# Convolution and state-space heads on one core: a 64x64 transform in array tiles, with shared rings and a written-out order

## The chip, the cores and the metric

The kernel runs on one core of a Trainium2 chip. The metric is device time in microseconds (us), from start to end of one launch; smaller is better. A core has five engines that run side by side: TensorE (PE in the profile; PEld is its loading of weights), VectorE (DVE), ScalarE (ACT), GpSimd (POOL) and SyncE (SP). In this kernel the last two issue nearly all DMAs. Matmuls write to PSUM, which has eight banks of 128 x 512 fp32 here; ACT and DVE bring the results from there to SBUF.

## The reference

Two independent heads, each on a sequence of S = 2048 positions and D = 1024 channels, in bf16. Their results stand side by side in the output.

```python
# head A
k_shift = sum over t < 4 of k_pad[:, t:t+S, :] * shift_k[:, 3 - t]
kv = k_shift * v
y = irfft(rfft(kv, 2S) * rfft(ssm_k, 2S))[:S] + kv * ssm_D
a = q * y
# head B
Lam_bar = exp(dt * Lam);  Bu = x @ B_bar.T          # complex
h[t] = Lam_bar * h[t-1] + Bu[t]
b = 2 * real(h @ Cmat.T) + x * Dskip
```

## The kernel before, in words

**Head B** works through 16 chunks i of 128 positions. `U(i, jp)` (L579, matmuls at L588) makes a quarter of Bu with 32 matmuls of 128x128 by 128x128 on PE; `ue` (L590) copies it out on ACT. On DVE a chunk then goes through `r1` (L600, rotation by a table, into the product tile mt), `r2` (L609, L611, adds, and the carry from the chunk before), `sc` (two scans at L618, and the next carry at L622 and L623), `r3` (L600 again, rotation back) and `r4` (L630). `y(i, dh, part)` (L634, matmuls at L641, skip term at L646) multiplies with C in eight parts, two halves dh of four, each half in one PSUM bank; `ye` (L656) and `yst` (L658) copy and store it. The chain over the chunks is sequential on DVE through the carry. Before the first U all of B must be loaded (`bl`, L556), transposed on PE (`bT`, L553) and copied (`bc`, L564); C likewise (`cl`, `cT`, `cc`, L572) before the first y. `x` (L576) loads a chunk of x through a transposing DMA.

**Head A** is a 4096-point transform split as 256 x 16, in three stages with a round trip through DRAM between each two.

- Stage 1, 16 residues n2. `k` (L660) and `v` (L670) load one residue, 128 rows 16 positions apart, with one DMA of 256 KB each; `kvm` and `kva` (L675 to L691) form kv on DVE; `am(n2, w)` (L695, L698) multiplies by the constant F1t in four matmuls 128x128 by 128x512; `ae` (L707) copies; `ast` (L709) stores 256 KB to Ys_kv. For ssm_k the same: `hl`, `hT` (L722), `hc` (L730), `hd`, `hm` (L742, two matmuls of 256 columns), `he` (L750), `hst` (L757) into Ys_h.
- Stage 2, 32 groups g. `l` (L760) loads two groups of both spectra and their weight tile wts, all in one step, into a ring of three (`l2`). `sh` and `sk` (L772) transform, `she` (L779) and `ske` (L785) copy, `sw` (L790, L791) swaps real and imaginary halves by two SBUF-to-SBUF DMAs, `pr` (L796) multiplies, `sa` (L805) transforms back, `sae` (L817) copies, `vst` (L819) stores to Vs.
- Stage 3, 16 residues. `vl` (L824) loads both halves of Vs, `ql` (L829) q, `a3` (L836) is four matmuls 128x128 by 128x512, `a3e` (L844) copies, `qm` (L848) multiplies by q, `ost` (L850) stores.

Every load of spectra in stage 2 waits for all of stage 1's stores; every `vl` waits for all `vst`.

**What sets the order.** `make_plan` (L174) lists each step as a task with an engine, a duration, dependencies, buffers taken and given back, and a due time `pr`. `Plan.run` (L88) plays this through and gives the list in which the steps are emitted. Each engine and each DMA queue then runs its own part of that list strictly in order.

**Buffers.** PSUM is split into four pools: ps_t 2 banks, ps_u 2, ps_y 1, ps_a 3. SBUF has a pool per kind of tile (for example u 5, xT 8, h 2, ld 5, ysb 3, hab 4, vv 4), some of them opened only for their stage, and one product tile mt that `r1`, `r3` and `kvm` share.

Of the kernel before, what the change touches and what calls it, by code (L numbers as in the profile page):

```python
# [15 lines left out]
F32 = mybir.dt.float32  # L16
# [5 lines left out]
N1, N2, NFFT = 256, 16, 4096  # L22
NG = 32


def a_constants():
    n1 = np.arange(128)[:, None]; k1 = np.arange(128)[None, :]
    ang = 2 * np.pi * n1 * (k1 + 0.5) / N1
    F1 = np.stack([np.cos(ang), -np.sin(ang)], axis=1)
    G = np.stack([np.cos(ang.T) * 2 / NFFT, -np.sin(ang.T) * 2 / NFFT], axis=1)  # L30
    s = np.arange(4)[:, None, None, None]; g = np.arange(NG)[None, :, None, None]
    n2 = np.arange(N2)[None, None, :, None]; k2 = np.arange(N2)[None, None, None, :]
    kk1 = 32 * s + g
    phi = 2 * np.pi * n2 * (2 * kk1 + 1 + 2 * N1 * k2) / (2 * NFFT)
    cph, sph = np.cos(phi), np.sin(phi)
    W2 = np.zeros((2, 4, N2, NG, 2, 4, N2))
    Wa = np.zeros((2, 4, N2, NG, 2, 4, N2))
    Wb = np.zeros((2, 4, N2, NG, 2, 4, N2))
    for si in range(4):
        c_ = cph[si]; s_ = sph[si]  # L40
        c_n2k2 = np.transpose(c_, (1, 0, 2)); s_n2k2 = np.transpose(s_, (1, 0, 2))
        W2[0, si, :, :, 0, si, :] = c_n2k2
        W2[1, si, :, :, 0, si, :] = s_n2k2
        W2[0, si, :, :, 1, si, :] = -s_n2k2
        W2[1, si, :, :, 1, si, :] = c_n2k2
        c_k2n2 = np.transpose(c_, (2, 0, 1)); s_k2n2 = np.transpose(s_, (2, 0, 1))
        Wa[0, si, :, :, 0, si, :] = c_k2n2
        Wa[0, si, :, :, 1, si, :] = s_k2n2
        Wa[1, si, :, :, 0, si, :] = -c_k2n2
        Wa[1, si, :, :, 1, si, :] = -s_k2n2  # L50
        Wb[0, si, :, :, 0, si, :] = -s_k2n2
        Wb[0, si, :, :, 1, si, :] = c_k2n2
        Wb[1, si, :, :, 0, si, :] = -s_k2n2
        Wb[1, si, :, :, 1, si, :] = c_k2n2
    f = lambda a: np.ascontiguousarray(a.reshape(128, -1), dtype=np.float32).astype(ml_dtypes.bfloat16)
    W2 = np.transpose(W2, (0, 2, 1, 3, 4, 5, 6))
    Wa = np.transpose(Wa, (0, 1, 2, 3, 4, 6, 5))
    Wb = np.transpose(Wb, (0, 1, 2, 3, 4, 6, 5))
    W3 = np.stack([W2.reshape(128, NG, 128), Wa.reshape(128, NG, 128), Wb.reshape(128, NG, 128)], axis=2)
    return f(F1), f(G), f(W3)  # L60


class Task:
    __slots__ = ("name", "eng", "dur", "lat", "deps", "acq", "rel", "pr", "idx", "nd", "succ", "after", "asucc", "t0", "t1", "nbytes")


COLD = 14.0
LAT = {"PE": .25, "ACT": .2, "DVE": .15, "SP": 0.0, "POOL": 0.0}


class Plan:
    def __init__(self, caps, rate=310e3, dlat=1.6):
        self.T, self.order, self.caps, self.rate, self.dlat = {}, [], dict(caps), rate, dlat

    def add(self, name, eng, dur, deps=(), acq=(), rel=(), pr=0.0, nbytes=0, after=None):
        assert name not in self.T, name
        t = Task()
        t.name, t.eng, t.dur, t.pr, t.nbytes = name, eng, dur, pr, nbytes
        t.deps = [d for d in deps if d is not None]
        t.acq = [(a, 1) if isinstance(a, str) else a for a in acq]  # L80
        t.rel = [(a, 1) if isinstance(a, str) else a for a in rel]
        t.lat = LAT[eng]
        t.after = after
        t.idx = len(self.order)
        self.T[name] = t
        self.order.append(t)

    def run(self):  # L88
        for t in self.order:
            t.succ, t.asucc, t.nd = [], [], len(t.deps) + (t.after is not None)  # L90
        for t in self.order:
            for d in t.deps:
                self.T[d].succ.append(t)
            if t.after is not None:
                self.T[t.after].asucc.append(t)
        free = dict(self.caps)
        engs = list(LAT)
        et = {e: 0.0 for e in engs}
        avail = {e: [] for e in engs}
        ev, seq, now, dma_free, done, started = [], 0, 0.0, 0.0, 0, []  # L100
        for t in self.order:
            if t.nd == 0:
                heapq.heappush(avail[t.eng], (t.pr, t.idx, t))
        while done < len(self.order):
            progress = True
            while progress:
                progress = False
                for e in engs:
                    if et[e] > now + 1e-9:
                        continue  # L110
                    h, skipped, t = avail[e], [], None
                    while h:
                        it = heapq.heappop(h)
                        if all(free[a] >= n for a, n in it[2].acq):
                            t = it[2]
                            break
                        skipped.append(it)
# [187 lines left out]
def full_kernel(ctx, tc, A_q, A_k, A_v, A_shift_k, A_ssm_k, A_ssm_D, B_x, B_Lre, B_Lim, B_Bre, B_Bim,  # L305
# [13 lines left out]
    GC = 2  # L319
# [592 lines left out]
```

## Time and profile before

| what | value |
|---|---|
| timed runs | 398.64, 402.03, 404.80 us; median 402.03 |
| the profiled execution | span 401.5 us from first to last instruction, 9098 instructions; no separate time is given for it |
| mean granted TensorE clock | 0.992 |
| DMA, whole span | 101.15 MB, 252 GB/s |
| q1 (issued by SP) | 57.17 MB, 47.3% of 16 engines' span |
| q0 (issued by POOL) | 43.40 MB, 31.2% of 16 engines' span |
| first vl issued | 339.2 us |
| last matmuls (y) | end 395.77 us (393.66 + 2.11) |

The page gives busy time by engine, the span in 40 slices, the chain of work that ended last, and the costliest groups of instructions. A group's line shows source line, engine, operation, output and input tile and shape, then the total and mean duration, then the idle time of its engine just ahead of it. Matmuls are pipelined: the mean duration of one is longer than the distance from one to the next. A table of windows gives each engine's busy microseconds in a stretch of the span, with the number of instructions in brackets.

### The profile page before, as it was taken

The page shows a single profiled execution, that of the slowest core. Times are in us where ns is not written, and L with a number is a line of the kernel's source. Part 1 is how long each engine was busy: PE and PEld are TensorE (multiplying, and loading weights), DVE is VectorE, ACT ScalarE, POOL GpSimd, SP SyncE. Part 2 cuts the span into 40 slices and gives each one's busy share as a digit, 9 for nine tenths or more (in the row PEclk, how much of TensorE's full clock was granted, in tenths as well). Part 3 has the DMA queues.
Part 4 walks back from the last instruction along what each step waited for, and adds up shares of the span by engine and source line. Part 5 has one row for each costly group of instructions (what it writes and reads, how often), then busy time and mean ns, then how long its engine had stood idle before and what let it go on. Part 6 is the DMA issues. An engine that isn't in the chain of part 4 may idle for free.

```text
span 401.5 us, 9098 instructions
## 1 busy us (share of the span) xinstructions
PE 366.2 (91%) x3593; PEld 248.6 (62%) x3593; DVE 336.4 (84%) x338; ACT 291.6 (73%) x527; POOL 132.1 (33%) x228
## 2 busy tenths in 40 slices
PE   3589989998999999896989999798999999999994
PEld 0489988977668778582544465563655457667441
DVE  7695589998799999999779999984969894969861
ACT  6598989999797887642778976588778883453542
POOL 7002243435465564511333332224222431021121
PEclk9999999999999999998999999999999999999998
DMA  6999799698888463468599994998698553999982
GB/s 181 278 270 303 254 309 326 194 358 308 284 287 234 137 221 97 157 175 327 133 318 289 326 293 61 305 320 282 214 335 270 185 145 144 338 368 330 335 282 106
DMA packets 55132, 101.15 MB, mean 252 GB/s; under 512 B 23204, under 2 KB 25252, under 8 KB 55089
## 3 DMA queue, kind: packets, MB, share of 16 engines
q1 hardware_dynamic: 40864, 57.17, 47.3%
q0 software_dynamic: 14224, 43.40, 31.2%
q8 instruction: 28, 0.46, 0.5%
q14 instruction: 16, 0.12, 0.1%
HBM read 54.41 MB, written 33.55 MB: 219 GB/s over the span
## 4 chain that ended last, share of the span: by engine, by line
PE 42%; DMA 15%; issue 14%; DVE 13%; ACT 9%; POOL 4%; SPq 2%; POOLq 0%; ACTq 0%; DVEq 0%
PE ps_y L641 14%; PE ps_u L588 12%; PE ps_a L805 5%; PE ps_a L772 5%; DMA wts<-a_c_W 4%; DMA hab<-hab 3%; DVE h L618 3%; DMA Ys_kv<-ysb 3%; DVE hab L796 2%; DMA Ys_h<-ysbh 2%; DMA ld<-in_B_B_re_dram 2%; ACT ysbh L750 2%; POOL out_dram L850 2%; PE ps_a L698 1%; POOL Ys_h L757 1%
## 5 line engine op out<-in xcount | busy, mean ns | idle before, releaser
L641 PE MATMUL ps_y<-CT,h 128*128 128x512 bf16 x512 | 138.1, 381 | 3.6 <-ACT yo L656 1.6
L588 PEld LDWEIGHTS <-BT 128*128 128x128 bf16 x2048 | 120.8, 99 | 9.0 <-issue 1.5
L588 PE MATMUL ps_u<-xT,BT 128*128 128x128 bf16 x2048 | 126.0, 221 | 0.1
L641 PEld LDWEIGHTS <-h 128*128 128x128 bf16 x512 | 47.0, 98 | 50.8 <-DVE h L630 2.5
L618 DVE TENSOR_TENSOR_SCAN h<-rtab,h 128x1024 bf16<-128x1024 f32 x32 | 71.5, 2276 | 0.3
L590 ACT CAST u<-ps_u 128x512 bf16<-128x512 f32 x64 | 37.9, 604 | 41.9 <-PE ps_u L588 41.8
L757 POOL DMA_DIRECT2D Ys_h<-ysbh x64 | 46.2, 724 | 38.8 <-ACT ysbh L750 38.7
L796 DVE TENSOR_TENSOR hab<-x,hab 128x2048 bf16<-128x2048 bf16 x32 | 38.5, 1221 | 14.8 <-ACT hab L779 6.5
L600 DVE TENSOR_TENSOR mt<-u,Z 128x4096 bf16<-128x4096 bf16 x16 | 36.6, 2289 | 11.2 <-ACT u L590 11.0
L779 ACT CAST hab<-ps_a 128x512 bf16<-128x512 f32 x64 | 36.2, 600 | 10.8 <-DMA l2h<-Ys_h 5.7
L790 POOL DMA_DIRECT2D hab<-hab x32 | 16.8, 526 | 76.3 <-ACT hab L779 64.7
L817 ACT CAST vsb<-ps_a 128x512 bf16<-128x512 f32 x64 | 34.7, 596 | 9.7 <-PE ps_a L805 6.2
L785 ACT CAST x<-ps_a 128x512 bf16<-128x512 f32 x64 | 36.9, 599 | 5.2 <-PE ps_a L772 5.0
L750 ACT CAST ysbh<-ps_a 128x512 bf16<-128x512 f32 x64 | 36.8, 637 | 4.3 <-DMA Ys_h<-ysbh 2.6
L707 ACT CAST ysb<-ps_a 128x512 bf16<-128x512 f32 x64 | 36.0, 629 | 5.2 <-DMA Ys_kv<-ysb 1.6
L805 PE MATMUL ps_a<-hab,wts 128*128 128x512 bf16 x128 | 33.5, 380 | 4.0 <-DVE hab L796 3.2
L600 DVE TENSOR_TENSOR mt<-h,Z 128x4096 bf16<-128x4096 bf16 x16 | 36.5, 2283 | 0.0
L709 POOL DMA_DIRECT2D Ys_kv<-ysb x32 | 17.9, 559 | 53.4 <-ACT ysb L707 53.3
L681 DVE TENSOR_TENSOR mt<-kring,wbc 128x4096 bf16<-128x4096 bf16 (+3 forms) x16 | 30.2, 1886 | 0.1
L553 PE MATMUL ps_t<-ident,ld 128*128 128x128 bf16 x256 | 21.1, 233 | 9.2 <-DMA ld<-in_B_B_re_dram 5.8
L646 PE MATMUL ps_y<-Dd,xT 128*128 128x128 bf16 x128 | 28.0, 219 | 0.0
L772 PE MATMUL ps_a<-l2h,wts 128*128 128x512 bf16 x64 | 21.9, 386 | 5.6 <-DMA wts<-a_c_W 5.4
(117 smaller groups left out, 473.4 us busy)
## 6 DMA issues: line engine op xcount, KB each, us to landing
Ys_kv<-ysb POOLq DMA_DIRECT2D x32, 256.0 KB, 3.8
Ys_h<-ysbh POOLq DMA_DIRECT2D x64, 128.0 KB, 3.3
l2h<-Ys_h SPq DMA_DIRECT2D x16, 512.0 KB, 5.9
l2k<-Ys_kv SPq DMA_DIRECT2D x16, 512.0 KB, 8.2
hab<-hab POOLq DMA_DIRECT2D x64, 128.0 KB, 4.1
Vs<-vsb POOLq DMA_DIRECT2D x16, 512.0 KB, 7.2
vv<-Vs SPq DMA_DIRECT2D x32, 256.0 KB, 5.0
hk<-in_A_ssm_k_dram SPq DMA_DIRECT2D x8, 512.0 KB, 7.2
```

What stands on the lines that cost most here:

```text
L588: nc.tensor.matmul(pu[:, w, jl, :], BT[:, 2 * jp + jl, w, d, :], xT[:, d, :], start=(d == 0), stop=(d == ND - 1))
L590: E["ue"] = lambda i, jp: nc.scalar.copy(st["u", i][:, :, 2 * jp:2 * jp + 2, :], st.pop(("pu", i, jp))[:])
L600: nc.vector.tensor_mul(m, s_, win(Z))
L618: nc.vector.tensor_tensor_scan(gf[:, a * W:(a + 1) * W], rt1, gf[:, a * W:(a + 1) * W], 0.0, ALU.mult, ALU.add)
L641: nc.tensor.matmul(py[:], h[:, 1 - w, j, :], CT[:, j, w, dh * 512:(dh + 1) * 512], start=(j == 0 and w == 0), stop=(j == NJ - 1 and w == 1))
L750: nc.scalar.copy(st["yh", qd, n4, w // 2][:, :, w % 2, :], st.pop(("pa", qd, n4, w))[:].rearrange("p (c d) -> p c d", c=2))
L757: gpd(Ys_h[cc, n0:n0 + 2, :, qd * DQ:(qd + 1) * DQ].rearrange("n k d -> k n d"), t_[:, cc, :, :])
L772: nc.tensor.matmul(st["ps", nm, g, w][:], st["w", gq][:, gi, 0, :], st[nm, gq][:, gi, w * 512:(w + 1) * 512], start=True, stop=True)
L779: nc.scalar.copy(st["hab", g][:, 0, w * 512:(w + 1) * 512], st.pop(("ps", "l2h", g, w))[:])
L785: nc.scalar.copy(st["x16", g][:, w * 512:(w + 1) * 512], st.pop(("ps", "l2k", g, w))[:])
L796: nc.vector.tensor_mul(hab[:], st.pop(("x16", g))[:].unsqueeze(1).to_broadcast([P, 2, D]), hab[:])
L805: nc.tensor.matmul(pt[:], st["w", gq][:, gi, 1 + a, :], hab[:, a, w * 512:(w + 1) * 512], start=(a == 0), stop=(a == 1))
```

## The change

1. **The transform is split 64 x 64.** Partitions of head A's outer stages hold four quarters of the residues, 32 rows each. Stage 1 for kv is one step `am(n2)` of eight matmuls 32x64 by 32x512, written to four PSUM banks, at the four row and two column positions of the array. Stage 3, `a3(n2)`, is eight matmuls 64x32 by 64x512 at two row and four column positions, into two banks. The kernel spectrum's `hm` keeps two matmuls of 256 columns with a zero-padded constant. Stage 2 keeps its counts and shapes, with other constants.
2. **Loads by quarters.** k, v, q and head A's output move in pairs of residues, by four DMAs of 32 partitions each (runs of 4 KB in place of 2 KB). `ast` is two DMAs of 128 KB with runs of 1 KB in place of one with 2 KB; `vl` two of 256 KB with runs of 1 KB.
3. **Rings.** All eight PSUM banks form one ring. SBUF tiles of 2 KB a partition share ring K2 (13 tiles), those of 4 KB ring K4 (12). The weights of stage 2 have a ring of three and a step of their own (`lw`), and the loads of the two spectra are separate steps (`lh` waits only for Ys_h, `lk` only for Ys_kv).
4. **Two product tiles** mt in place of one.
5. **Order.** Planner and costs are gone; a list ORDER of all steps is in the file. The loads of B come first, k and v later; the chunks' U are not in order of i (5, 8, 7, 9, 11, 6, 10, 12, 14, 13, 15).

```diff
-N1, N2, NFFT = 256, 16, 4096
+N1, N2, NFFT = 64, 64, 4096
+NR = 16
...
+CFG = {'ps': 8, 'mt': 2, 'K2': 13, 'K4': 12, 'wts': 3, 'l2h': 3, 'l2k': 3, 'kr': 8, 'bdve': 4, 'actsw': ()}
...
+ORDER = """
+ld_par ld_w ld_G bl.7.0 ld_F lw.2 bl.6.1 bl.4.0 ld_sd wb.0 bl.5.0 bl.3.0 par_T wbe.0 bl.6.0 wb.1 p32 lw.1 bT.7.0 exp1 hl.0.0 wbe.1 dve2 hl.0.1 wb.4
...
+kva.12 U.6.1 ue.9.2 kva.13 U.6.2 ue.6.1 am.12 ue.6.2 U.6.3 kvm.14 ae.12.2 ae.12.0 ae.12.1 ae.12.3 am.13 ast.12.0 ue.6.3 kvm.15 U.7.1 ae.13.0 ae.13.2
+ast.12.1 ae.13.3 U.7.2 ae.13.1 kva.14 ast.13.1 ue.7.1 lh.1 lh.0 lh.2 ast.13.0 U.7.3 ue.7.2 kva.15 am.14 ue.7.3 U.11.2 ae.14.0 ae.14.1 sc.5 ae.14.2
...
+sae.26.1 y.10.1.0 sae.27.0 sae.27.1 U.15.0 r2.13 vst.13 y.10.1.1 sc.13 ue.15.0 y.10.1.2 qp.3 U.15.1 vl.0 U.15.2 ue.15.1 r3.13 y.10.1.3 ue.15.2 U.15.3
+vl.1 ye.10.1 yst.10 r4.13 y.11.0.0 ue.15.3 r1.15 a3.0 y.12.0.0 vl.2 y.11.0.1 a3e.0.0 y.11.0.2 a3e.0.1 a3.1 qm.0 y.11.0.3 vl.3 a3e.1.0 a3e.1.1 y.11.1.0
...
+a3.14 ye.15.1 a3e.14.0 a3e.14.1 a3.15 qm.14 a3e.15.0 a3e.15.1 yst.15 qm.15 yst.14 op.7
+"""
...
+    def rows2(dma, t_, src, r2, load=True):
+        for qt in range(4):
+            a, b = t_[32 * qt:32 * qt + 32, :, :], src[:, qt, 2 * r2:2 * r2 + 2, :]
+            dma(a, b) if load else dma(b, a)
...
-    def ptile(pool, shape, dt_=F32):
-        return psum[pool].tile(shape, dt_, name=pool)
+    def ptile(name, shape, dt_=F32):
+        return psum.tile(shape, dt_, name=name, tag="ps", bufs=c["ps"])
...
-    def am(n2, w):
-        cc, dh = divmod(w, 2)
-        st["pa", n2, w] = ptile("ps_a", [P, 512])
-        nc.tensor.matmul(st["pa", n2, w][:], F1t[:, cc, :], st["kv", n2][:, dh * 512:(dh + 1) * 512], start=True, stop=True)
+    def am(n2):
+        kv = st.pop(("kv", n2))
+        for w in range(4):
+            st["pa", n2, w] = ptile("ps_a", [P, 512])
+        for dh in range(2):
+            for w in range(4):
+                b = 32 * w
+                nc.tensor.matmul(st["pa", n2, w][64 * dh:64 * dh + 64, :], F1t[b:b + 32, :], kv[b:b + 32, dh * 512:(dh + 1) * 512],
+                                 start=True, stop=True)
...
+    def ast(n2, w):
+        t_ = st.pop(("ysb", n2, w))
+        for dh in range(2):
+            gpd(Ys_kv[n2, 2 * w:2 * w + 2, :, dh * 512:(dh + 1) * 512].rearrange("q k d -> k q d"), t_[64 * dh:64 * dh + 64, :, :])
...
-        for nm, Ys in (("l2h", Ys_h), ("l2k", Ys_kv)):
-            st[nm, gq] = a2.tile([P, GC, D], BF16, name=nm, bufs=c["l2"])
-            spd(st[nm, gq][:], Ys.rearrange("c n (s g) d -> (c n s) g d", g=NG)[:, gq * GC:(gq + 1) * GC, :])
-        st["w", gq] = a2.tile([P, GC, 3, P], BF16, name="wts", bufs=c["l2"])
-        spd(st["w", gq][:], W3v[:, gq * GC:(gq + 1) * GC, :, :])
+    def lw(gq):
+        st["w", gq] = ring.tile([P, GC, 3, P], BF16, name="wts", tag="wts", bufs=c["wts"])
+        spd(st["w", gq][:], W3v[:, gq * GC:(gq + 1) * GC, :, :])
...
     def vl(n2):
-        for cc in range(2):
-            spd(st["vv", n2][:, cc, :], Vs[cc, n2, :, :])
+        st["vv", n2] = k4("vv", [P, 4, 512])
+        for dh in range(2):
+            spd(st["vv", n2][64 * dh:64 * dh + 64, :, :], Vs[n2, :, :, dh * 512:(dh + 1) * 512].rearrange("q k d -> k q d"))
...
+    def a3_(n2):
+        vv = st.pop(("vv", n2))
+        for w in range(2):
+            st["po", n2, w] = ptile("ps_a", [P, 512])
+        for qt in range(4):
+            for w in range(2):
+                nc.tensor.matmul(st["po", n2, w][32 * qt:32 * qt + 32, :], Gt[64 * w:64 * w + 64, :], vv[64 * w:64 * w + 64, qt, :],
+                                 start=True, stop=True, tile_position=(64 * w, 32 * qt))
...
     with tc.manual_schedule():
-        for t in make_plan(c).run():
-            E[t.name[0]](*t.name[1:])
+        for t in ORDER.split():
+            f, *a = t.split(".")
+            E[f](*map(int, a))
```

## The prediction, made before the run

> **What bounds the kernel now.** I read the page's busy line first, then the 40 slices, then a table of windows, then the chain. The page:
>
> ```profile
> PE 366.2 (91%) x3593; PEld 248.6 (62%) x3593; DVE 336.4 (84%) x338; ACT 291.6 (73%) x527; POOL 132.1 (33%) x228
> ...
> PE   3589989998999999896989999798999999999994
> ...
> DVE  7695589998799999999779999984969894969861
> ...
> DMA  6999799698888463468599994998698553999982
> ```
>
> No engine is full, but PE and DVE are near it, and the DMA row is at 9 at both ends. So I cut the span at 103 us and at the first load of stage 3 (339.2 us). Columns: stretch, its length, then busy us of PE, PEld, DVE, ACT, POOL, then PE clock, DMA share, GB/s.
>
> ```profile
> 0.00:103.00 103.00, 86.21 (x1162) 74.47 (x1163) 82.89 (x129) 90.19 (x150) 36.23 (x62) 1.00 0.91 280
> 103.00:339.20 236.20, 224.06 (x1980) 141.09 (x1979) 209.49 (x170) 174.96 (x330) 85.00 (x146) 0.99 0.73 230
> 339.20:401.50 62.30, 55.93 (x457) 33.08 (x454) 44.01 (x41) 26.47 (x48) 10.82 (x20) 0.98 0.82 288
> ```
>
> First stretch: DMA-bound (91%, 28.8 MB at 280 GB/s). Second: PE-bound, 224 of 236, DVE next with 209. Third: PE-bound again. Busy overstates a matmul's cost, so I take paces from the chain (start, duration, what) and durations from the groups:
>
> ```profile
> 214.70 0.86 PE ps_y L641 x4
> ...
> 230.73 1.79 PE ps_u L588 x32
> ...
> 249.49 10.91 DMA wts<-a_c_W
> ```
>
> ```profile
> L698 PE MATMUL ps_a<-acc,F1t 128*128 128x512 bf16 x64 | 20.3, 379 | 0.6 <-DVE acc L691 0.3 <-ACT ysbh L750 0.3
> ...
> L836 PE MATMUL ps_a<-vv,Gt 128*128 128x512 bf16 x64 | 17.2, 379 | 0.0
> ```
>
> A 512-column matmul lasts 379 ns but follows the last after 0.86/4 = 0.215 us; a 128-column one after 1.79/32 = 0.056 us. The chain also shows a weight tile of stage 2 that was 10.9 us on its way while PE had little else.
>
> [...]
>
> **Array tiles.** Removed: 64 matmuls at L698 and 64 at L836, in 16 + 16 visits of four: 0.86 us a visit, 27.5 us in all. Added: 32 visits of eight small matmuls. Not in the trace, so bounds: [...] all eight in turn, 8 x 0.215 = 1.73 us. I take 0.57[...]. That is 18.2 us for 32 visits: PE saves 9.3 us[...]. Weight loads (eight of 32 or 64 columns against 98 ns for 128) are hidden in it, or in the upper bound.
>
> **The other engines** do the same work. DVE: same rows, 336 us. ACT: same evictions, 292. POOL: 32 more `ast`, 16 more `op` DMAs and one more constant, 8 fewer loads of k and v: 41 x 0.55 = +23 us, hidden in 269 us of idle time. SP: 60 more issues (k 27, v 17, q 16) at 0.43 = 26 us on a queue of some 180 issues; a blocked load there holds up all behind it, which the shared rings make possible, and I charge it below. Bytes stay near 101 MB; 16.8 MB (k, v, q, output) go in 4 KB runs in place of 2 KB, 16.8 MB (`ast`, `vl`) in 1 KB.
>
> **The new order, stretch by stretch.** I lay the durations of the groups (paces for PE) along ORDER and add them up to three places. Group means overlap, so DVE sums are scaled by 336.4/349.2 = 0.963 and ACT's by 291.6/321.9 = 0.906, so that they meet the page.
>
> | up to | PE | DVE | ACT | MB issued |
> |---|---|---|---|---|
> | r1.3 | 88.0 | 84.0 | 90.2 | 28.6 |
> | vl.0 | 301.7 | 301.2 | 268.0 | 85.4 |
> | end | 351.9 | 336.4 | 291.6 | 100.6 |
>
> *To r1.3.* 28.6 MB at the 280 GB/s of the first stretch: 102 us. The old kernel had done the same by then (86.2 PE, 82.9 DVE, 90.2 ACT, 28.8 MB), so B first gains nothing here: DVE idles early (25 us of it stand before r1.0, which ACT's 36.1 x 0.906 = 33 us of copies and tables let start near 37), and the loads of k and v are merely later.
>
> *r1.3 to vl.0.* PE 213.7, DVE 217.2: DVE is now the longer. The old kernel paid 236.2 - 224.1 = 12 us over its longer engine. Of that I strike what the waits view names and the change takes up: PE on late wts 5.4 (own ring and step), PE's ps_y on the copy to yo 1.4 (one PSUM bank there, now eight shared). Left: 5. Sum 222. Two product tiles let DVE run the next multiply ahead of the last add, but save it no work. The round trip after stage 1 (`ast` landing 4.3, `lk` 8.2, `sk` and copies 2 us, some 17 with stage 1's last evictions) lies beside sc.5, r1.6, r3.5, r4.5, r1.7, r2.6 and sc.6 on DVE, 19 us, and beside U, y and `sh` on PE. With that cover gone it would cost its 17 us.
>
> *vl.0 to the end.* PE 50.2 (y of five chunks, the end of U, 16 visits), DVE 35, 15.2 MB / 338 GB/s (the rate of 340 to 380 us) = 45. PE sets it: 50, and after the last matmul 8 us (old: 401.5 - 395.8 = 5.7, and now a copy, `qm` and four issues at 0.54 for the last pair). 58.
>
> Sum: 102 + 222 + 58 = **382 us**, against the profiled span of 401.5, which lies 0.5 under the median of 402.03. So I make no correction.
>
> **Rivals.**
> - *Fast.* Tiles at 0.30 a visit, and 4 KB runs lift the first stretch to what PE and DVE need, 97 (84 + 12 before r1.0, 87 + 10 on PE); DVE's 217 without waits; tail 46 + 8. Sum 368. For: the sums of PE, DVE, ACT and the DMAs in each stretch lie close together, so none has to run far ahead. Against: an in-order list meets waits somewhere.
> - *The tail becomes a DMA bound.* If `vl`'s 1 KB runs move at half the rate, 8.4 MB / 169 + 6.8 / 338 = 70 us in place of 50: 402. It decides from 280 GB/s downward. For: DMA is at 95% or more from 340 to 380 already. Against: stores with 512 B runs (Ys_h) land in 3.3 us.
> - *The tiles run one after another* (slower). At 1.73 us a visit PE has 227.6 us in the middle, longer than DVE, and 68.8 in the tail: 104 + 233 + 77 = 414. It decides where a visit costs over 1.4 us (no gain left), 1.7 for a loss over 2%. Against: the positions given are disjoint in rows and banks, so nothing in the program asks for turns. [...]
> - *Ring coupling.* A load waits on a slot whose store has not landed, and SP's queue behind it: three or four stalls of 5 us in the middle give 397.
>
> **How the numbers follow.** A change of 2% (8 us) is about what a measurement of this kernel can tell from none. Chances: the sum above 0.58 (372 to 394), fast 0.19 (358 to 372), DMA tail 0.11 (390 to 403), ring coupling 0.06, tiles in turn 0.06 (404 to 416). Faster by over 2% is below 394: nearly all of the first, the fast case, and some of the tail's: 0.82. Within 2%: 0.12. Slower: 0.06. The range leaves out the slow tiles and the ends of the others: 360 to 398; the likeliest case alone is 372 to 394.
>
> **What would show it.** Right: L549 and L699 in groups of eight with starts a few ns apart and some 0.5 to 0.6 us per visit; DVE at 90% or more from 103 us to the first vl near 324; no wait of PE on wts; PE without gaps in the tail. Wrong: visits of 1.5 us or more; vl landing in over 8 us with PE waiting on it; SP's queue waiting for store landings in the middle; a first r1.3 well before or after 102 us.

## The result and the profile after

The changed kernel is slower: a median of 416.69 us (416.23 to 418.22, 4 runs) against 400.57 for the kernel before in the same session, a ratio of 1.039 with a 95% interval of 1.031 to 1.047. The forecast of 382 us and its range of 360 to 398 both missed. Ratios, not microseconds, are what compares runs of different sessions, since the kernel before itself came out between 400.6 and 404.8 from one session to the next. Executions of one kernel fall into a faster and a slower state: the ratios and intervals here are of the faster ones of both kernels, the medians in us of all.

First the page of the changed kernel, the same rows as shown for the kernel before:

```profile
PE 361.6 (87%) x3721; PEld 241.8 (58%) x3721; DVE 334.7 (80%) x338; ACT 286.8 (69%) x527; POOL 157.1 (38%) x269
...
PE   5988899998999879997979977799699899899960
...
DVE  7574899898979997999966968699698999788420
...
DMA  7999999989765827648997999898989576899981
```

PE's work did shrink (366.2 to 361.6 us), but its row now has sixes and sevens in the middle, where before it had nines, and the DMA row has nines there. At the end, PE's row falls to 6 and 0. The table of windows, cut as in the prediction (at 103 us and at the first load of stage 3, now at 349.7):

```profile
0.00:103.00 103.00, 89.80 (x1102) 72.29 (x1103) 81.75 (x126) 84.92 (x139) 34.31 (x58) 1.00 0.98 276
103.00:349.70 246.70, 221.98 (x2232) 146.61 (x2231) 216.84 (x178) 177.59 (x344) 102.23 (x174) 0.99 0.80 234
349.70:416.40 66.70, 49.81 (x392) 22.92 (x389) 36.09 (x36) 24.26 (x46) 20.53 (x38) 0.92 0.81 229
```

The middle is 246.7 us long, with VectorE busy 216.8 and TensorE 222.0 of it: neither fills it. The tail is 66.7 us with 49.8 of TensorE. By engine, the chain of work that ended last now begins with transfers ("DMA 38%; PE 35%", before "PE 42%; DMA 15%"). Three of its pieces are weight tiles of stage 2, and two are array-tile visits (start, duration, what):

```profile
122.65 0.46 PE ps_a L549 x8
...
220.83 5.02 DMA wts<-a_c_W
241.22 11.95 DMA wts<-a_c_W
290.03 11.60 DMA wts<-a_c_W
...
379.75 0.80 PE ps_a L699 x16
```

Eight tiles take 0.46 us at L549, sixteen take 0.80 at L699: 0.40 to 0.46 a visit, where four matmuls took 0.86. In the trace the eight tiles of a visit start 3 or 4 ns apart (210 of the 224 distances), and in 12 of the 16 visits at L549 the next matmul starts 0.35 us after the first tile. The tiles work better than forecast. The waits from 190 to 350 us say what stage 2 stands for instead (engine, line, what it waited for: us in total, times, longest):

```profile
DVE hab L658 <- DMA hab<-hab: 10.9, 7, 3.6
...
PEld L628 <- DMA l2k<-Ys_kv: 6.8, 4, 2.4
...
PE ps_a L628 <- DMA l2k<-Ys_kv: 5.3, 4, 1.9
PEld L628 <- DMA wts<-a_c_W: 5.2, 3, 2.5
PE ps_a L628 <- DMA wts<-a_c_W: 4.2, 3, 2.2
```

All of these are transfers of stage 2. The weight load (PEld) and its matmul wait side by side, so only one of each pair counts. The lines left out are mostly engines that wait for each other; TensorE's largest is on VectorE's product (PEld L667, 12.7 us), which itself waits in part for the swaps of `hab`.

### The profile page after: what moved, and what is told of

Same layout as the page of the kernel before. It is cut to its first block, busy times and chain, and to the rows that moved or that the text cites. A ratio compares the mean times of both kernels' runs of the same rounds, so it can differ in the third digit from the quotient of the medians.

```text
span 416.4 us, 9530 instructions
## 1 busy us (share of the span) xinstructions
PE 361.6 (87%) x3721; PEld 241.8 (58%) x3721; DVE 334.7 (80%) x338; ACT 286.8 (69%) x527; POOL 157.1 (38%) x269
## 4 chain that ended last, share of the span: by engine, by line
DMA 38%; PE 35%; ACT 8%; issue 5%; POOL 5%; DVE 4%; SPq 2%; ACTq 0%; POOLq 0%; DVEq 0%
PE ps_u L430 13%; PE ps_y L483 8%; DMA vv<-Vs 7%; DMA wts<-a_c_W 7%; DMA Ys_h<-ysbh 7%; PE ps_a L667 5%; PE ps_a L628 4%; DMA l2k<-Ys_kv 4%; DMA out_dram<-yo 3%; DMA Ys_kv<-ysb 3%; DMA hab<-hab 3%; ACT ysbh L604 3%; POOL Ys_kv L562 2%; PE ps_t L394 2%; ACT ysb L556 2%
## 5 line engine op out<-in xcount | busy, mean ns | idle before, releaser
L430 PE MATMUL ps_u<-xT,BT 128*128 128x128 bf16 x2048 | 123.8, 220 | 5.8 <-ACT hT L584 2.4
L430 PEld LDWEIGHTS <-BT 128*128 128x128 bf16 x2048 | 118.8, 99 | 14.1 <-issue 9.5
L483 PE MATMUL ps_y<-CT,h 128*128 128x512 bf16 x512 | 126.3, 379 | 0.6 <-ACT CT L414 0.5
L483 PEld LDWEIGHTS <-h 128*128 128x128 bf16 x512 | 45.1, 98 | 47.1 <-issue 4.0
L658 DVE TENSOR_TENSOR hab<-x,hab 128x2048 bf16<-128x2048 bf16 x32 | 38.5, 1222 | 21.1 <-DMA hab<-hab 10.9
L432 ACT CAST u<-ps_u 128x512 bf16<-128x512 f32 x64 | 39.9, 633 | 17.6 <-PE ps_u L430 15.6
L562 POOL DMA_DIRECT2D Ys_kv<-ysb x64 | 38.4, 605 | 23.9 <-ACT ysb L556 23.8
L604 ACT CAST ysbh<-ps_a 128x512 bf16<-128x512 f32 x64 | 35.1, 648 | 8.2 <-DMA Ys_h<-ysbh 5.5
L556 ACT CAST ysb<-ps_a 128x512 bf16<-128x512 f32 x64 | 34.1, 619 | 8.7 <-DMA out_dram<-yo 3.1
L498 ACT CAST yo<-ps_y 128x512 bf16<-128x512 f32 x32 | 19.3, 608 | 30.2 <-PE ps_y L483 29.5
L667 PE MATMUL ps_a<-hab,wts 128*128 128x512 bf16 x128 | 33.0, 380 | 7.0 <-DVE hab L658 6.8
L707 ACT CAST ot<-ps_a 128x512 bf16<-128x512 f32 x32 | 16.9, 595 | 17.9 <-PE ps_a L699 9.8
```

The source lines that it names most:

```text
L430: nc.tensor.matmul(pu[:, w, jl, :], BT[:, 2 * jp + jl, w, d, :], xT[:, d, :], start=(d == 0), stop=(d == ND - 1))
L432: E["ue"] = lambda i, jp: nc.scalar.copy(st["u", i][:, :, 2 * jp:2 * jp + 2, :], st.pop(("pu", i, jp))[:])
L483: nc.tensor.matmul(py[:], h[:, 1 - w, j, :], CT[:, j, w, dh * 512:(dh + 1) * 512], start=(j == 0 and w == 0), stop=(j == NJ - 1 and w == 1))
L556: nc.scalar.copy(st["ysb", n2, w // 2][:, w % 2, :], st.pop(("pa", n2, w))[:])
L562: gpd(Ys_kv[n2, 2 * w:2 * w + 2, :, dh * 512:(dh + 1) * 512].rearrange("q k d -> k q d"), t_[64 * dh:64 * dh + 64, :, :])
L604: nc.scalar.copy(st["yh", qd, n4, w // 2][:, :, w % 2, :], st.pop(("pa", qd, n4, w))[:].rearrange("p (c d) -> p c d", c=2))
```

## The experiments

Eighteen kernels, in the order in which the question changed. In the expectations, theory P is that the pieces of the transform (quarters, 1 KB runs) cost the time, theory O that the order and the rings lose it.

### Pieces or order: four variants of the changed kernel

Run 1 (e1_old_transform) keeps the rings, the two product tiles and the written order, and puts back the 256x16 transform with its layouts and single DMAs. Run 3 (e3_vl_runs) only changes the load of stage 3. Run 4 (e4_one_dma) loads and stores two rows by one DMA in place of four quarters. Run 2 (e2_all_large) does 3 and 4 and stores `ast` in one run for each partition. Runs 2 to 4 move the same bytes to other places. In this order:

```diff
-N1, N2, NFFT = 64, 64, 4096
+N1, N2, NFFT = 256, 16, 4096
...
-        for qt in range(4):
-            for w in range(2):
-                nc.tensor.matmul(st["po", n2, w][32 * qt:32 * qt + 32, :], Gt[64 * w:64 * w + 64, :], vv[64 * w:64 * w + 64, qt, :],
-                                 start=True, stop=True, tile_position=(64 * w, 32 * qt))
+        for w in range(2):
+            for cc in range(2):
+                nc.tensor.matmul(st["po", n2, w][:], Gt[:, cc, :], vv[:, cc, w * 512:(w + 1) * 512], start=(cc == 0), stop=(cc == 1))
```

```diff
-            spd(st["vv", n2][64 * dh:64 * dh + 64, :, :], Vs[n2, :, :, dh * 512:(dh + 1) * 512].rearrange("q k d -> k q d"))
+            spd(st["vv", n2][64 * dh:64 * dh + 64, :, :].rearrange("p a b -> p (a b)"),
+                Vs[n2].rearrange("q k d -> (q k d)").rearrange("(p e) -> p e", p=P)[64 * dh:64 * dh + 64, :])
```

```diff
-        for qt in range(4):
-            a, b = t_[32 * qt:32 * qt + 32, :, :], src[:, qt, 2 * r2:2 * r2 + 2, :]
-            dma(a, b) if load else dma(b, a)
+        a, b = t_, nat[id(src)][:, 2 * r2:2 * r2 + 2, :]
+        dma(a, b) if load else dma(b, a)
```

```diff
-            gpd(Ys_kv[n2, 2 * w:2 * w + 2, :, dh * 512:(dh + 1) * 512].rearrange("q k d -> k q d"), t_[64 * dh:64 * dh + 64, :, :])
+            gpd(Ys_kv[n2, 2 * w + dh, :, :], t_[64 * dh:64 * dh + 64, :, :].rearrange("p a b -> p (a b)"))
```

> The kernel after, with its rings, its two product tiles and its order, but the 256 x 16 transform of before: am and a3 are again four matmuls 128x128 by 128x512, k, v, q and the output go in one DMA per pair of residues (128 partitions, 4 KB runs), ast and vl have 2 KB runs. Theory P (pieces: the 1 KB runs and the quarters cost DMA time, 315 us of engine-time before and 350 after for the same bytes): about 395, below before, since the order's gain shows once the pieces are gone. Theory O (the order and the rings lose the time): 415 to 430, since nothing of the loss goes and PE gets 14 us more work.

> The kernel after with larger pieces everywhere: vl in runs of 4 KB, ast in runs of 2 KB, k, v, q and the output in one DMA per pair of residues. The rows then hold other data, so head A's result is not the reference's; bytes, matmuls, order and rings are those of after. Theory P: 395 or less, the first vl near 335 and a tail of 58. Theory O: 410 to 417.

> The kernel after with vl alone in runs of 4 KB instead of 1 KB (rows hold other data, so head A's result is not the reference's). Theory P for the tail: vl lands in 5 us instead of 6.7, the tail falls from 66.7 to 58, 408 in all. Rival (the tail is bound by the bytes or by PE): no change, 416.

> The kernel after with k, v, q and head A's output in one DMA of 512 KB per pair of residues in place of four of 128 KB (partitions hold other residues, so head A's result is not the reference's). Theory P: 405 or less if the quarters cost the time. Rival (quarters are only issue time on idle queues): within 3 us of 416.7.

Measured for runs 1 to 4: 413.1 (ratio 1.029, interval 1.024 to 1.034), 413.9 (1.022, 1.010 to 1.033), 414.3 (1.029, 1.021 to 1.037) and 413.7 us (1.028, 1.021 to 1.035). Against 1.039 each takes 1.0 to 1.7% off, their intervals still overlap that of the changed kernel (1.031 to 1.047), and none comes near the kernel before. With the old transform, the new order and rings still lose about 3%, some 12 us. Theory P falls as the main cause in the changed kernel.

### The other corner, the end, and the transfers of stage 2

Run 5 (e5_tiles_old_order) puts the array tiles under the planner, pools and single product tile of the kernel before:

```diff
-        for w in range(4):
-            A(("am", n2, w), "PE", .216, [("kva", n2), ("ld_F",)], ["ps_a"], ["acc"] if w == 3 else [], pr=p + 3)
+        for h in range(2):
+            A(("am", n2, h), "PE", .3, [("kva", n2), ("ld_F",)], [("ps_a", 2)], ["acc"] if h == 1 else [], pr=p + 3)
...
-            A(("a3", n2, w), "PE", .432, [("vl", n2), ("ld_G",)], ["ps_a"], ["vv"] if w == 1 else [], pr=p)
+        A(("a3", n2), "PE", .432, [("vl", n2), ("ld_G",)], [("ps_a", 2)], ["vv"], pr=p)
```

Run 6 (e6_end_on_sp) is the changed kernel with its last stores on SP:

```diff
-    E["yst"] = lambda i: gpd(out_b[i * T:(i + 1) * T, :], st.pop(("yo", i))[:])
+    E["yst"] = lambda i: (spd if i >= 14 else gpd)(out_b[i * T:(i + 1) * T, :], st.pop(("yo", i))[:])
...
-    E["op"] = lambda r: rows2(gpd, st.pop(("ot", r)), oar, r, False)
+    E["op"] = lambda r: rows2(spd if r >= 6 else gpd, st.pop(("ot", r)), oar, r, False)
```

Runs 7 (e7_no_swaps_after) and 8 (e8_no_swaps_before) leave the swaps of `hab` out of either kernel:

```diff
-        gpd(hab[0:64, 1, :], hab[64:128, 0, :])
-        gpd(hab[64:128, 1, :], hab[0:64, 0, :])
...
-        nc.vector.tensor_mul(hab[:], st.pop(("x16", g))[:].unsqueeze(1).to_broadcast([P, 2, D]), hab[:])
+        x16 = st.pop(("x16", g))
+        nc.vector.tensor_mul(hab[:, 1, :], x16[:], hab[:, 0, :])
+        nc.vector.tensor_mul(hab[:, 0, :], x16[:], hab[:, 0, :])
```

> The other corner of the two-by-two: the 64x64 transform with array tiles (first stage in two visits of four tiles and two banks, last stage in one visit of eight), its layouts in DRAM and its 1 KB runs, under the planner, the pools and the single product tile of the kernel before. Rows are loaded and stored by one DMA each, so they arrive in another permutation; the amount of work is that of the real one. Theory O (order and rings lose the time): the kernel before keeps TensorE busy to the end, so what the tiles save there is gained: 16 visits of 0.40 us instead of 0.86 in the tail are 7 us, the first stage is worth 0 to 4; 391 to 397 us, 0.97 to 0.99 of before. Theory P (the pieces of the transform cost it): its 1 KB loads and stores cost here what they cost in the new order, about 4 us; 403 to 407.

> The changed kernel with its last stores (outputs of rows 12 to 15 of A and the last two of B) issued by SP instead of GpSimd. Theory D (GpSimd's last drain grows with the small stores queued just ahead of it): the drain falls from 9.0 us to about 4, the time by 4 to 5, to 412. Rival: the end waits for the last bytes whoever issues them; the drain falls but SP's wait takes its place, 415 to 417.

> The changed kernel without the 64 DMAs that swap the halves of hab in stage 2 (8.4 MB inside SBUF); the product then reads the unswapped half twice, in two instructions, so head A's result is another. Theory T (in the new order stage 2 is bound by transfers: 264 GB/s at a share of 0.91 from 200 to 345): about 25 us of the 16 engines' time go, stage 2 shortens by 8 to 15 us and the time falls to 402 to 409. Rival R (the ring slots, SP waiting in order for them, set stage 2): 413 to 417, as loads come when slots come free.

> The same taken out of the kernel before, whose TensorE idles 7 us between 190 and 350. Theory T: it gains less than the changed kernel does, 1 to 5 us, 396 to 400. Rival R: both gain alike.

Run 6: 410.0 us, ratio 1.015 (1.009 to 1.021), so about 2% comes back. GpSimd ends its program with a drain, an instruction that stands in the trace but that the page does not count. In the changed kernel it lasted 9.0 us, from 406.6 to 415.7, though the last byte had moved by 409.3. With the last stores on SP it lasted 10.1 us, but from 390.7 to 400.9, beside the last loads and matmuls, and the program ended 1.3 us after the last byte. So the drain was moved out of the way; it was not shortened, which is what theory D expected. From the last matmul to the end 13.3 us became 6.3.

The drain was 4.0 us in the profile of the kernel before and 7.6 in run 8, which ends with the same stores, so the small stores alone don't set its length; what does stays open. It also enters the comparisons above: from the last matmul to the end, runs 1 to 4 took 6.8, 8.4, 13.4 and 10.0 us. In their profiles, runs 1, 2 and 4 gain no more over the changed kernel (5.0, 3.6 and 2.8 us of the span) than this end is shorter (6.5, 4.9 and 3.3 us), so their gain can't be put down to larger pieces.

Runs 7 and 8: 397.9 us (0.988, 0.982 to 0.994) and 402.6 (0.997, 0.994 to 1.000). The same 8.4 MB cost the changed kernel 5% and the kernel before nothing that can be told. The drain blurs both figures. Without the swaps the first `vl` comes 12.5 us earlier in the profile of the changed kernel and 6.4 in that of the kernel before; at the end, a drain 4.0 us shorter adds to the first gain and one 3.5 us longer takes from the second. The windows from 190 to 300 us, first the changed kernel, then run 7 (columns as above):

```profile
190.00:300.00 110.00, 94.60 (x664) 51.13 (x664) 90.50 (x72) 77.69 (x154) 34.73 (x66) 0.98 0.94 269
```

```profile
190.00:300.00 110.00, 105.50 (x808) 59.90 (x816) 106.70 (x106) 88.48 (x178) 13.42 (x24) 0.98 0.80 251
```

And the same for the kernel before, then run 8:

```profile
190.00:300.00 110.00, 103.75 (x789) 58.59 (x788) 93.09 (x73) 84.71 (x163) 33.48 (x63) 1.00 0.84 259
```

```profile
190.00:300.00 110.00, 107.37 (x813) 61.54 (x825) 103.36 (x106) 88.26 (x171) 9.66 (x18) 1.00 0.65 213
```

With the 16 DMA engines at 94%, TensorE is idle 15 us and VectorE 20; with the swaps gone, the DMA share falls to 80% and they are at 96 and 97%. In the kernel before, these 110 us have TensorE busy 103.8 at a DMA share of 0.84, and 107.4 without the swaps. So stage 2 of the changed kernel is bound by its transfers, and that of the kernel before rather by TensorE. One thing these two runs do not separate: they take away the bytes of the swaps and also a step that each product waits for (a swap landed in 6.2 us in the changed kernel, in 4.1 in the kernel before).

Run 5 contradicts what theory O said of it: 415.0 us, 1.030 (1.024 to 1.036). The tiles lose in the old order too, but elsewhere: up to 350 us TensorE had been busy 321.1 us in run 5 and in the kernel before alike. The loss is in the tail: of 12.8 us between the two spans, 5.2 stand after the last matmul, where the drain took 7.8 us. The rest is taken up further below.

### Filling or emptying stage 2

Theory Y: the new order leaves too much of y for the tail. Run 10 (e10_y_earlier) moves the y tasks of chunks 10 and 11, with their evictions and stores, into stage 2:

```diff
-... y.9.1.3 ... y.10.0.0 ... y.10.0.3 ... y.10.1.0 ... vl.0 ... y.10.1.3 ... y.11.0.0 ... y.11.1.3 ...
+... y.9.1.3 ... y.10.0.0 ... y.10.1.3 ... r4.11 ... y.11.0.0 ... y.11.1.3 ... vl.0 ...
```

Run 11 (e11_pool_swaps) is run 6 with the swaps done by GpSimd:

```diff
-        gpd(hab[0:64, 1, :], hab[64:128, 0, :])
-        gpd(hab[64:128, 1, :], hab[0:64, 0, :])
+        nc.gpsimd.tensor_copy(hab[0:64, 1, :], hab[64:128, 0, :])
+        nc.gpsimd.tensor_copy(hab[64:128, 1, :], hab[0:64, 0, :])
```

Run 12 (e12_act_swaps_y) is runs 6 and 10 together, with `actsw` holding every third group, so that ScalarE does 11 of the 32 swaps in its evictions:

```diff
-... 'actsw': ()}
+... 'actsw': tuple(range(0, 32, 3))}
...
     def sw(g):
+        if g in c["actsw"]:
+            return
```

> The changed kernel with 16 y tasks (chunks 10 and 11, 15 us of TensorE) and their evictions and stores moved from around and behind the start of the last stage into stage 2, where TensorE idles 15 us between 190 and 300 and 3 us between 300 and 350. Theory Y (the new order leaves too much of y for the tail): the first load of the last stage moves by under 5 us and the time falls by 4 to 10, to 407 to 412. Rival: the idle time of stage 2 lies where these tasks cannot go, so they push stage 2 back by what they take from the tail, 415 to 418.

> The changed kernel with its last stores on SP (410.0 by itself) and the swaps of hab done by two copies on GpSimd in place of two DMAs, so that the result stays the kernel's. Theory T: the transfers fall as in the run without swaps, which gained 18 us; with copies of under 2 us each on an engine that is idle most of the stage, 393 to 402. Rival: GpSimd's copies take 3 us or more, or hold VectorE up; the swap is then later than by DMA, 408 or more.

> The changed kernel with its last stores on SP, the y tasks earlier, and 11 of the 32 swaps done by ScalarE's evictions (two more of 64 rows for each half) in place of DMAs. Theories T and Y together: 2.9 MB less in stage 2 are worth a third of the 18 us, the y tasks 4 to 10; 396 to 403. If ScalarE's 22 us more bind stage 2, or the y tasks only move the wait: 405 to 411.

Measured: 423.9 us (1.053, 1.045 to 1.061), 441.4 (1.098, 1.087 to 1.109), 419.5 (1.041, 1.031 to 1.050). Runs 10 and 12 came out worse than either side of their expectations. Theory Y falls: in run 10 TensorE had been busy 312.1 us up to 350, as in the changed kernel, and the last store of Vs was issued at 352.7 in place of 344.4. The y tasks did not fill idle time, they pushed stage 2 back. The engines ran their lists in order: in the trace of the changed kernel 212 groups of TensorE's matmuls and 216 of ScalarE's copies come in the sequence of ORDER. So where an engine idled it stood behind an instruction that waited, and work placed behind that one did not use the gap. Run 11's price is in its groups (busy us, mean ns, then idle time ahead of it):

```profile
L652 POOL COPY hab<-hab 64x1024 bf16<-64x1024 bf16 x32 | 71.2, 2223 | 12.7 <-ACT hab L638 11.2
L653 POOL COPY hab<-hab 64x1024 bf16<-64x1024 bf16 x32 | 68.1, 2129 | 1.3
L658 DVE TENSOR_TENSOR hab<-x,hab 128x2048 bf16<-128x2048 bf16 x32 | 48.2, 1532 | 7.9 <-POOL hab L653 7.8
```

A swap by two copies takes 4.4 us of GpSimd, and VectorE's products beside it rise from 1222 to 1532 ns. Run 12 mixes three edits, of which run 10 alone accounts for a loss; it is no measure of the ScalarE swaps.

### Why the tiles lose in the old order: transfers into half of the partitions

In run 5 the tail's transfers went at 270 GB/s with the engines always busy, against 346 in the kernel before. Run 9 (e9_old_order_vl_runs) gives it the 8 KB runs of run 3. Run 14 (e14_vl_all_partitions) cuts stage 3's load by quarter, each DMA into all partitions, and run 15 (e15_vl_all_long_runs) makes it one DMA of 8 KB runs:

```diff
-        for dh in range(2):
-            spd(st["vv", n2][64 * dh:64 * dh + 64, :, :], Vs[n2, :, :, dh * 512:(dh + 1) * 512].rearrange("q k d -> k q d"))
+        for q in range(4):
+            spd(st["vv", n2][:, q, :], Vs[n2, q].rearrange("k (h d) -> h k d", h=2))
```

```diff
+        spd(st["vv", n2][:].rearrange("p a b -> p (a b)"),
+            Vs[n2].rearrange("q k d -> (q k d)").rearrange("(p e) -> p e", p=P))
```

Run 16 (e16_vl_all_end_sp) is the changed kernel with the loads of run 14 and the end of run 6.

> The tiles under the old order once more, with the loads of the last stage's products as one contiguous piece of 8 KB in place of four runs of 1 KB in each partition (so other elements land in each partition; work and bytes are the same). In the run before it, after 344 us, the 16 engines were busy all the time (share 1.09) but moved 265 GB/s where the kernel before moves 350. Theory P2 (the 1 KB runs are what binds the tail once its work is short): the 8.4 MB cost 7 to 10 us less, 400 to 407. Rival B (the last stage wants two banks at once, and its outputs' ring of three waits for stores): 411 to 416.

> The tiles under the old order (415.0) with the last stage's loads cut the other way: four DMAs for each tile, one for each quarter, each into all 128 partitions, in place of two that each fill 64 partitions; every piece stays 1 KB. Theory H (a transfer into half of the partitions runs at a lower rate: with runs of 8 KB into 64 partitions the hardware queue's 4 KB packets took 258 ns in the tail where 159 is the median elsewhere): the tail's packets get faster and the time falls by 5 or more, to 402 to 410. Theory P2 (1 KB pieces cost it): 413 to 417.

> The same with one DMA of 8 KB runs into all 128 partitions (other elements land in each partition; bytes are the same). Theory H: 4 KB packets near 160 ns, a tail at 350 GB/s as in the kernel before, 398 to 405. If 64 or 128 partitions make no difference, 412 to 416 as with the 8 KB runs into 64 partitions.

> The changed kernel with both of these: the last stage's loads into all partitions in four DMAs of 1 KB runs, and its last stores on SP (410.0 by itself). Theory H: the waits of TensorE on these loads (11 us in the changed kernel) fall by half or more, 404 to 408. Otherwise 409 to 411.

Run 9: 414.0 us, 1.027 (1.020 to 1.035): longer runs alone mend nothing, so P2 falls. Run 15: 408.0 us, 1.014 (1.010 to 1.018). The tail from 350 to 380 us, in run 9 and then in run 15:

```profile
350.00:380.00 30.00, 25.47 (x276) 15.21 (x281) 23.26 (x21) 11.62 (x22) 4.86 (x9) 0.94 1.04 289
```

```profile
350.00:380.00 30.00, 28.16 (x312) 16.77 (x310) 28.81 (x26) 13.76 (x26) 5.95 (x11) 1.00 0.97 354
```

The same runs of 8 KB, the same bytes: 289 GB/s into 64 partitions at a time, 354 into 128. The median 4 KB packet of SP's queue between 344 and 392 us took 258 ns in run 9 and 159 in run 15. In the last stage of runs 2 and 3, whose loads also fill 64 partitions, it took 236 and 199. Theory H had asked for packets near 160 ns and a tail at 350 GB/s, and both came (159 ns, 354 GB/s), though the time of 408.0 us lies above its 398 to 405. It holds as far as these two runs go; why half of the partitions are slower, no run shows. Run 15 also has one DMA where run 9 has two; their number was not tested apart.

Runs 14 and 16 went to 553.1 and 549.1 us (1.360 and 1.347), for a reason that I had not thought of. Run 14's loads, durations at SP as minimum, median and maximum:

```profile
L827 SPq DMA_DIRECT2D vv<-Vs x64: 494/2631/3503, 341.9 to 526.9; - x64
```

They take 185 us. Their 1 KB packets took 46 ns at the median (79 in run 5, but 52 in the changed kernel, also into 64 partitions, so the partitions alone don't set this time), and 8192 x 0.046 = 377 us of them in 185 us is the work of two DMA engines and not of the page's sixteen. What held them to that was not tested: against run 15, run 14 differs in the length of its runs, in the number of its DMAs and in the order of the source's dimensions at once. So what 1 KB runs into all partitions would give over 16 engines was not measured.

### What makes stage 2 crowded

In the kernel before the first load of `l2k` was issued at 176.7 us, in the changed kernel at 200.2, with the last of A's products on VectorE at 169 and 190. The first load of stage 3 followed at 339.2 and 349.7. In the kernel before, then in the changed one (minimum, median and maximum ns, first and last start):

```profile
L691 DVE TENSOR_TENSOR acc<-acc,ld x16: 691/691/693, 29.9 to 168.3; 128x1024 bf16<-128x1024 bf16 x16
...
L764 SPq DMA_DIRECT2D l2k<-Ys_kv x16: 319/426/1039, 176.7 to 306.2; - x16
...
L824 SPq DMA_DIRECT2D vv<-Vs x32: 319/429/1515, 339.2 to 379.9; - x32
```

```profile
L536 DVE TENSOR_TENSOR acc<-acc,v x16: 691/692/693, 70.3 to 189.2; 128x1024 bf16<-128x1024 bf16 x16
...
L621 SPq DMA_DIRECT2D l2k<-Ys_kv x16: 319/320/742, 200.2 to 312.4; - x16
...
L685 SPq DMA_DIRECT2D vv<-Vs x32: 573/580/1302, 349.7 to 396.0; - x32
```

So stage 2 itself is not longer than before. From the first load of `l2k` to the first `vl` it takes 162.5 us in the kernel before and 149.5 in the changed one, which starts it 23.5 us late and ends it 10.5 us late. TensorE has less to do beside it (busy 133.0 us in place of 151.8), but the transfers don't let it go faster: the same stretch is 145.3 to 151.1 us in runs 1 to 4 and 6, and 135.0 in run 7, which leaves the swaps out. From 186 to 340 us the DMA view counts 37.25 MB before and 40.49 after. Run 13 (e13_products_earlier) moves five steps of the B chain (and y of chunk 4) behind A's products:

```diff
-... sc.4 ... r1.5 ... r2.5 ... r3.4 ... r4.4 ... y.4.0.0 ... kva.15 ...
+... kva.15 sc.4 r3.4 r4.4 r1.5 r2.5 ... y.4.0.0 ...
```

> The changed kernel with five steps of the B chain (scan 4, its two steps after, and the two of chunk 5 ahead of scan 5; 12 us of VectorE) moved from among the last products of A behind them, with the y tasks of chunk 4. In the changed kernel the last product ended at 190 us and the first load of l2k was issued at 200.2; in the kernel before at 169 and 176.7, so that 16 loads of l2k fall into 112 us instead of 129. Theory K (the late end of the products crowds stage 2's transfers): the first l2k load comes at about 189, the last store of Vs 5 to 10 us earlier, the time 407 to 412. Rival: stage 2 takes its transfers' time wherever it starts, or the chain's delay comes back at the end: 415 to 422.

421.6 us in its fastest execution and 430.2 to 431.5 in the three others, of which the profile is one; there is no ratio for it. Even the fastest is not below the changed kernel. The move did not do what it was for: in the profile the last product ended at 192 us, no earlier, the first load of `l2k` came at 214.6, and VectorE was busy 30.0 of the 40 us from 150 to 190 (before the move 35.9). So theory K was not put to the test. From the waits of run 13 between 140 and 200 us:

```profile
DVE acc L568 <- DMA Ys_h<-ysbh: 9.0, 1, 9.0
...
DVE acc L568 <- DMA Ys_kv<-ysb: 5.1, 1, 5.1
```

`acc` does not read these stores. It wants a slot of the 2 KB ring, and the slot's last user, a `ysb` or `ysbh`, has not landed in DRAM. That is the coupling of the rings, between an operation and a stranger's store. In the kernel before, `acc` had buffers of its own. How long these two waits are may belong to that one execution; in the profile of the changed kernel the same two are 3.2 and 2.7 us. So the last two runs: run 17 (e17_one_more_slot) is run 6 with one more slot, and run 18 (e18_old_order_full_rate) is run 15 with its last six stores on SP.

```diff
-CFG = {'ps': 8, 'mt': 2, 'K2': 13, ...
+CFG = {'ps': 8, 'mt': 2, 'K2': 14, ...
```

```diff
+    E["yst"] = lambda i: (spd if i >= 14 else gpd)(out_b[i * T:(i + 1) * T, :], st.pop(("yo", i))[:])
+    E["ost"] = lambda n2: (spd if n2 >= 12 else gpd)(oar[:, n2, :], st.pop(("ot", n2))[:])
```

> The changed kernel with its last stores on SP (410.0 by itself) and 14 slots of 2 KB in the shared ring in place of 13. Ring theory (the rival of the prediction at 397: work waits for a slot whose store has not landed; the trace shows 24 us of such waits of VectorE and ScalarE between 60 and 200, 3 us in the kernel before, and in the run with the products earlier VectorE stood 9.0 and 5.1 us for one): the waits fall by a third or more, the products end by 2 to 5 us earlier, 405 to 408. If the slots cost nothing on the path: 409 to 411.

> The tiles under the old order with the 8 KB runs into all 128 partitions (408.0; its TensorE ended at 391 us, 6 before the kernel before does, but GpSimd's drain took 7.8 us) and the last six stores issued by SP. Theories H and D together: the end comes 2 to 3 us after the last byte (396), 400 to 403 in the median, below the kernel before by 1 to 3. If the drain is not what the end waits for: 406 to 409.

Run 17: 401.65 us, 0.997 (0.994 to 1.001), against 1.015 (1.009 to 1.021) for run 6. One slot of 2 KB is worth 1.8%, some 7 us. The products' last step, the loads of `l2k` and the stores of Vs (minimum, median and maximum ns, first and last start), in run 6 and then in run 17:

```profile
L536 DVE TENSOR_TENSOR acc<-acc,v x16: 691/691/693, 71.1 to 188.3; 128x1024 bf16<-128x1024 bf16 x16
...
L621 SPq DMA_DIRECT2D l2k<-Ys_kv x16: 319/320/562, 199.6 to 308.1; - x16
...
L680 POOL DMA_DIRECT2D Vs<-vsb x16: 537/554/564, 218.7 to 342.4; - x16
```

```profile
L536 DVE TENSOR_TENSOR acc<-acc,v x16: 691/692/692, 69.8 to 182.5; 128x1024 bf16<-128x1024 bf16 x16
...
L621 SPq DMA_DIRECT2D l2k<-Ys_kv x16: 319/320/1066, 193.6 to 304.7; - x16
...
L680 POOL DMA_DIRECT2D Vs<-vsb x16: 537/554/564, 215.0 to 336.6; - x16
```

Read downwards: the last product 5.8 us earlier, the first load of `l2k` 6.0 (the last one 3.4), the last store of Vs 5.8, and the span 6.9 (406.9 to 400.0). The head start reaches the end, and stage 2 takes 148.3 us where run 6 has 148.0. Both expectations for run 17 were too cautious. The waits of VectorE and ScalarE for stores between 60 and 200 us fall from 24 to 10 us in sum; in the kernel before they were 2.6.

Run 18: 401.5 us, 0.996 (0.992 to 0.999). With both faults away, the tiles under the old order are level with or just below the kernel before, not faster by the 9 us that the forecast gave the tiles. (TensorE ended at 391.9 us in run 15, which is 4 us before the 395.8 of the kernel before and not the 6 of the expectation.) Since the kernel before was not run with its last stores on SP, how much of that is the tiles' stays open. Neither run 17 nor run 18 beats the kernel before by what a comparison here can tell; and in run 18 elements lie in other places.

## Why the prediction was wrong

- **To r1.3, 102 us: right.** The multiply of chunk 3 starts at 102.75, with the DMA share at 0.98: bound by transfers, as forecast.
- **The visit of eight tiles, 0.57 us: too dear.** The 0.57 was my estimate; the trace of the kernel before has no array tile in it. In the chain it is 0.40 to 0.46. At the chain's pace 32 visits save 32 x (0.86 - 0.43) = 13.8 us of TensorE where I had 9.3. The rival of tiles in turn (414 us) landed near the result by accident: a visit would have had to cost 1.73 us.
- **r1.3 to vl.0, 222 us: the step that failed.** VectorE's work was 216.8 us, the forecast 217.2. The term that broke is the 5 us of waits left over VectorE's work: it is 246.7 - 216.8 = 30, of which 7.6 stand before 190 us and 22 in stage 2. I had struck TensorE's 5.4 us of waits on late weights because `wts` got its own ring and step. They stayed (4.2 us on the matmuls, with tiles 5 to 12 us on their way), TensorE's waits on `l2k` (5.3 us, none before) came on top, and VectorE's on the swaps rose from 4.9 to 10.9: the transfers of stage 2 were now the bound, and a ring of their own did not bring the weights forward. I had also held stage 1's round trip to be covered, and never asked when A's products end. They end 21 us later than before, and all 16 loads of `l2k` come after. Runs 7, 8 and 17 show the two parts: the transfers (5% without the swaps) and the ring (1.8% for one slot). I expect that the two overlap, since an earlier start is also room for transfers; they were not run together.
- **vl.0 to the end, 58 us: 66.7.** TensorE's part was right (49.8 against 50.2). The last matmul ended at 403.1, so 13.3 us followed it where I had 8; GpSimd's drain of 9.0 in place of 4.0 is the difference, and run 6, with 6.3, shows it. The rest is gaps of TensorE, 3.6 us of them on `vv`.
- **The ring rival (397 us, chance 0.06)** named the right mechanism in the wrong place. I looked for SP standing on store landings. In fact VectorE and ScalarE stood, up to 3 us at a time, in stage 1. Its chance was too small: a shared ring of 13 that serves eight kinds of tiles deserved to be counted through, by who held each slot before.
- **The DMA tail rival (402 us)** did not decide the changed kernel. The rate from 350 to 380 us, 230 GB/s, was below the 280 that I had set for it, and the chain that ended last runs through loads of `vv` from 370 us on (6.6 to 8.2 us each), but TensorE stood only those 3.6 us for them. In the old order, with the drain, it is what makes the tiles lose, by half the partitions (414.0 us in run 9, 408.0 in run 15) and not by 1 KB (415.0 in run 5, 414.0 in run 9).

Cut at 103.0 and 349.7 us, the error sums up: 1.0 + 24.7 + 8.7 = 34.4 us above 382, which is the span of 416.4. Of the 16 us over the kernel before, runs 6 and 17 give back all (1.039 to 1.015 to 0.997). What remains against the forecast, some 18 us, lies in the middle stretch alone: run 17 takes 101.6 us to r1.3, 240.3 to its first `vl` and 58.1 to the end, where the forecast had 102, 222 and 58. I put it down to stage 2 still bound by transfers: the DMA share from 190 to 300 us is 0.93 in run 17 too. No run takes the swaps out of run 17, so that last step is argued and not shown. The ring has a part in the late end of the products (one more slot ended them 5.8 us earlier). That the order with B first makes up the rest is inferred from the two timelines; run 13, meant to test it, did not end them earlier.

## What to carry to other kernels

Before joining buffers into one ring, list for each slot what frees it: a slot last read by a store to DRAM comes free when that store lands, and the next user, on whatever engine, inherits that wait (9.0 and 5.1 us of VectorE in run 13). When an order is rewritten, follow the last producer of each stage to the first load of the next: here stage 2 took some 145 to 151 us of transfers whether it began at 194 or at 202 us, and a late start went on to the end. Try a load that fills all 128 partitions against one that fills half of them: here the rate in the tail rose from 289 to 354 GB/s (runs 9 and 15, the latter with one DMA in place of two). Then look at how many DMA engines' work its packets are in the time it takes: in run 14, which also filled all 128, they were two's (377 us in 185 us). And when a change ends in other stores, compare the time from the last matmul to the end before crediting the rest.

## What the hardware showed that I had not expected

- 4 KB packets took 258 ns into 64 partitions and 159 into 128, in the same tail with the same runs (runs 9 and 15).
- The loads of run 14 took 185 us for 8.4 MB, with 377 us of packets: the pace of two DMA engines. What held them to it was not tested.
- Where GpSimd issued the last stores, its drain at the end lasted between 4.0 us (the kernel before) and 9.0 us (the changed kernel, where it ended at 415.7 us and the last byte had moved by 409.3); with the last stores on SP the end came 1.2 to 1.3 us after the last byte (runs 6, 17, 18).
- A visit of eight array tiles with 512 columns amid matmuls of the full array took 0.40 to 0.46 us in the chain, and 0.35 us from its first start to the next matmul's in 12 of the 16 visits at L549, where four full matmuls took 0.86 (the changed kernel and the kernel before).
- A copy of 64x1024 bf16 from one half of the partitions to the other took GpSimd 2.2 us, and with these copies VectorE's multiply in stage 2 rose from 1222 to 1532 ns on average (the changed kernel and run 11).
